# A gated mix of a spectral filter and a token MLP on one core: the row transform done first with x stationary, half the rows of the spectrum, the mirrored half made at the filter

## The chip, the cores and the metric

The kernel runs on one core of a Trainium2 chip. The metric is the time on the device in microseconds (us), the median of the runs shown. The core has five engines that each follow their own list of instructions in order and wait for one another through semaphores: TensorE (PE, with PEld for its weight loads), VectorE (DVE), ScalarE (ACT), GpSimd (POOL) and SyncE (SP, which issues all the loads and stores here).

## The reference

```python
g = sigmoid((x * gate_w).sum(-1, keepdims=True))
a = irfft2(rfft2(x) * (w_r + 1j * w_i))              # x: 1 x 2048 x 512, w: 2048 x 257
h = layernorm(x)                                     # over the 512 columns
u = gelu(einsum("bsd,sf->bdf", h, w1) + b1)          # w1: 2048 x 1792
b = (einsum("bdf,fs->bds", u, w2) + b2).transpose(0, 2, 1)
out = g * a + (1 - g) * b                            # 2048 x 512, bfloat16
```

The rows s (2048) are mixed by both parts: by the row transform of a, and by the two matrix products of b. Inputs and output are bfloat16.

## The kernel before, in words

Row s is split as 512q + 4a + r, with a on the 128 partitions, so that x is 16 tiles j = 4q + r of 128 x 512. The two products of the MLP are 14 blocks ft of 128 hidden units: `m1` (L462) sums 16 tiles of x into each block (224 matmuls of 128x512), GELU (L475, ACT) makes the block's activations `gl`, `m2` (L696) sums 14 blocks into each of the 16 output tiles (224 matmuls).

The spectral part is a chain of transforms beside this. For each tile, DVE folds x (`fold`, L361, L362), PE transposes it in 128x128 blocks (`tr`, L376), ACT copies the transposes out of PSUM (`tev`, L382), and PE transforms the columns (`f1`, L390). DVE makes the first radix-4 step over the rows (`radix4`, L413 to L429), PE makes the 128-point part (`f3`, L442 to L444), and a second radix-4 step gives the whole spectrum of 2048 x 256 in `Z`, in two halves h (even and odd columns). DVE multiplies by the complex filter (`mult`, L617 to L620). Columns 0 and 256 share a place, and POOL with three small matmuls takes them apart (`c0a`, `perm`, `c0b`, L520 to L609; 32 elements in a partition). Then the way back: radix-4, PE (`i1`, L637, L638), radix-4, and the column transform (`i3`, L665). ACT scales by the gate (L673, L675), and DVE adds to the MLP's output.

The order of all this is written out ahead of time. `Plan.order` takes each piece of work with an estimated duration, a priority and its inputs, plays it through, and the instructions are emitted in the resulting order. At run time each engine keeps that order: where a piece is late, all that stands behind it on its engine waits. In the priorities the spectral chain stands ahead of the MLP on PE, so that MLP matmuls fill the gaps. `m2` has four PSUM banks (`acc`). SP issues the loads in the plan's order, from eight that are under way at a time.

ACT loads a table of functions when it first needs one: for the copies, for Sqrt (`sq`, L346), for GELU and for Sigmoid (L491).

Of the kernel before, what the change touches and what calls it, by code (L numbers as in the profile page):

```python
# [16 lines left out]
P = 128  # L17
S = 2048
# [5 lines left out]
H = 128  # L24
# [6 lines left out]
def make_tables():  # L31

    p = np.arange(P)
    ident = np.eye(P)
    flip = np.zeros((P, P))
    flip[1:, 1:] = np.eye(P - 1)[::-1]
    e00 = np.zeros((P, P))
    e00[0, 0] = 1.0
    flip2 = np.eye(P)[::-1]
    small = bf(np.stack([flip, e00, flip2], 1))  # L40

    tf = np.zeros((P, 4, 2 * H))
    for kt in range(4):
        d = (kt % 2) * P + p[:, None]
        l = 2 * np.arange(H)[None, :] + kt // 2
        th = 2 * np.pi * ((d * l) % D) / D
        tf[:, kt, :H] = np.cos(th)
        tf[:, kt, H:] = -np.sin(th)
        if kt < 2:
            tf[:, kt, H] = np.where(d[:, 0] % 2 == 0, 1.0, -1.0)  # L50

    r4 = np.arange(4)
    ph = (4 * p[:, None, None, None] + r4[None, :, None, None]) * (r4[None, None, :, None] + 4 * p[None, None, None, :])
    th = 2 * np.pi * (ph % S) / S
    fwd = np.stack([np.cos(th), np.sin(th), -np.sin(th)], 3)
    thi = th.transpose(3, 1, 2, 0)
    inv = np.stack([-np.sin(thi), np.cos(thi), np.sin(thi)], 3)

    tg = np.zeros((P, 2, 2, 2 * H))
    sc = 2.0 / (D * S)  # L60
    for h in range(2):
        l = 2 * p[:, None] + h
        th = 2 * np.pi * ((l * np.arange(2 * H)[None, :]) % D) / D
        tg[:, h, 0] = sc * np.cos(th)
        tg[:, h, 1] = -sc * np.sin(th)
    tg[0, 0, 0] = sc / 2
    tg[0, 0, 1] = np.where(np.arange(2 * H) % 2 == 0, 1.0, -1.0) * sc / 2
    return {"ident": bf(ident), "small": small, "tf": bf(tf), "fwd": bf(fwd), "inv": bf(inv), "tg": bf(tg)}
# [123 lines left out]

@with_exitstack
def kernel(
# [25 lines left out]
    NWS = 7  # L220
    NT = 3
# [7 lines left out]
    caps = {"tp": 1, "fa": 3, "acc": 4, "xf": 2, "xT": 3, "w": NWS, "tb": NT}  # L229
# [6 lines left out]

    def load(key, shape, dt, src, nbytes, prio=0.0):
        def emit():
            t[key] = sb(shape, dt, key)
            dma(t[key][:], src)  # L240
        return add("SP", 0.2, emit, writes=[key], prio=prio, nbytes=nbytes)

    def alloc_first():
        t["x"] = sb([P, 4, 4, D], BF16, "x")
        t["h"] = sb([P, 4, 4, D], BF16, "h")
        t["xdt"] = sb([P, 4, 4, 2, 2, H], BF16, "xdt")
        t["fwd"] = sb([P, 4, 4, 3, P], BF16, "rot")
        t["Z"] = sb([P, 2, 4, 2, 4, H], BF16, "Z")
        t["gl"] = sb([P, NFT, D], BF16, "gl")
        t["pq"] = sb([P, 2048], BF16, "pq")  # L250
        t["st"] = sb([P, 2048], BF16, "st")
        t["wd"] = sb([P, 2, 2, NJ, H], BF16, "wd")
        t["wn"] = sb([P, 2, 2, NJ], BF16, "wn")
        t["wq"] = sb([P, 3, 4, 2, 2, 4], BF16, "wq")
        t["wp"] = sb([P, 2, 2, NJ], F32, "wp")
        t["wh"] = sb([P, 2, 2, NJ], F32, "wh")
        t["ghc"] = sb([P, 2, 2, NJ], F32, "ghc")
        t["u0"] = sb([P, 2, NJ], BF16, "u0")
        t["ur"] = sb([P, 2, 2, 4], BF16, "ur")
        t["us"] = sb([P, 3, 2, 4], BF16, "us")  # L260
        t["up"] = sb([P, 2, NJ], F32, "up")
        t["ct"] = sb([P, 4, 2, NJ], F32, "ct")
        t["consts"] = sb([P, 1], F32, "consts")
        for name, shape in (("stats", [P, NJ, nc.vector.BN_STATS_DIM]), ("mv", [P, NJ, nc.vector.BN_AGGR_DIM]),
                            ("rstd", [P, NJ]), ("glog", [P, NJ]), ("g", [P, NJ]), ("omg", [P, NJ]),
                            ("ombb2", [P, NJ]), ("b1f", [P, NFT]), ("b2f", [P, NJ])):
            t[name] = sb(shape, F32, name)
        V.memset(t["consts"][:], 1e-5)

    a0 = add("DVE", 0.1, alloc_first, writes=["consts"], prio=-1)  # L270


    def ld(key, dst, src, nbytes, prio):
        keys = key if isinstance(key, list) else [key]
        return add("SP", 0.2, lambda: dma(dst(), src), writes=keys, prio=prio, nbytes=nbytes, after=[a0])

    for r in range(4):
        for b in range(2 if r == 0 else 1):
            qs = slice(2 * b, 2 * b + 2) if r == 0 else slice(0, 4)
            ld([("x", r, b)] + ([("x", r, 1)] if r else []), lambda qs=qs, r=r: t["x"][:, qs, r, :], x4[:, qs, r, :],  # L280
               262144 if r == 0 else 524288, 2 * r + 0.1 * b)
# [12 lines left out]
    for r in range(4):  # L294
        for i in range(2):
            add("SP", 0.2, ld_w1(i, r), writes=[("w1", i, 4 * q + r) for q in range(4)], prio=2 * r + 0.5 + 0.1 * i,
                alloc=["w"] if r == 0 else (), nbytes=262144)
    load("ident", [P, P], BF16, tabs["ident"], 32768, prio=-1)
    load("tf", [P, 4, 2 * H], BF16, tabs["tf"], 262144, prio=0.3)
    load("small", [P, 3, P], BF16, tabs["small"], 98304, prio=14)  # L300
    for r in range(4):
        ld(("fwd", r), lambda r=r: t["fwd"][:, r, :, 0:2, :], tabs["fwd"][:, r, :, 0:2, :], 262144, 9 + r)
    load("b1b", [P, NFT], BF16, B_b1.rearrange("(t f) -> f t", f=P), 65536, prio=10.5)
    load("b2b", [P, 4, 4], BF16, B_b2.rearrange("(q a r) -> a q r", q=4, r=4), 16384, prio=10.6)
    load("gw", [P, D], BF16, gate_w[None, :].to_broadcast([P, D]), 131072, prio=13)

    def ld_wraw(comp):
        def emit():
            t["wraw", comp] = sb([P, 4, 4, 257], BF16, ("wraw", "wiaw")[comp])
            dma(t["wraw", comp][:], (A_w_r, A_w_i)[comp].rearrange("(e c k) l -> c e k l", e=4, k=4))  # L310
        return emit

    for i in range(2, NW):
        add("SP", 0.8, ld_w1(i, None), writes=[("w1", i, q) for q in range(NJ)], prio=11.5 if i == 2 else 18 + i, alloc=["w"],
            nbytes=1048576)
        if i in (3, 4):
            add("SP", 0.2, ld_wraw(i - 3), writes=[("wraw", i - 3)], prio=18.5 + i, nbytes=1056768)


    for r in range(4):  # L320
        xk = [("x", r, 0), ("x", r, 1)]
        js = [4 * q + r for q in range(4)]
        for b in range(2):
            jb = js[2 * b:2 * b + 2]

            def bn(jb=jb):
                for j in jb:
                    V.bn_stats(out=t["stats"][:, j, :], in_=t["x"][:, j // 4, j % 4, :])  # L328
                for j in jb:
                    V.bn_aggr(out=t["mv"][:, j, :], in_=t["stats"][:, j, :])  # L330
            add("DVE", 2 * (d1(512) + 0.09), bn, reads=[("x", r, b)], writes=[("mv", r, b)], prio=1.2 * r)

        def col(name, r, b):
            v = t[name][:].rearrange("p (q r) -> p q r", r=4)
            return v[:, b, r] if isinstance(b, slice) else v[:, 2 * b:2 * b + 2, r]


        for b in ((0, 1) if r == 0 else (slice(0, 4),)):
            bs = [b] if r == 0 else [0, 1]
            mvk = [("mv", r, c) for c in bs]  # L340
            rk = [("rstd", r, c) for c in bs]

            def sq(r=r, b=b):
                v = t["mv"][:].rearrange("p (q r) c -> p q r c", r=4)
                v = v[:, 2 * b:2 * b + 2, r, 1] if r == 0 else v[:, :, r, 1]
                A.activation(col("rstd", r, b), v, ActF.Sqrt, bias=t["consts"][:, 0:1], scale=1.0)  # L346
            add("ACT", 0.25, sq, reads=mvk + ["consts"], writes=rk, prio=-1)
            add("DVE", 0.12, lambda r=r, b=b: V.reciprocal(col("rstd", r, b), col("rstd", r, b)), reads=rk, writes=rk,
                prio=1.2 * r - 0.2)
        for q, j in enumerate(js):  # L350
            add("DVE", 0.32, lambda j=j: V.tensor_scalar(t["h"][:, j // 4, j % 4, :], t["x"][:, j // 4, j % 4, :], t["mv"][:, j, 0:1],
                                                         t["rstd"][:, j:j + 1], op0=Alu.subtract, op1=Alu.mult),
                reads=[("x", r, q // 2), ("rstd", r, q // 2), ("mv", r, q // 2)], writes=[("h", j)], prio=1.2 * r - 0.1)

        for b in ((0, 1) if r == 0 else (None,)):
            def fold(r=r, b=b):
                if not b:
                    t["xf", r] = t["gl"][:, 6 + 4 * (r % 2):10 + 4 * (r % 2), :].rearrange("p q (k d) -> p q k d", k=4)
# [418 lines left out]
```

## Time and profile before

| What | us |
|---|---|
| median of 3 runs (lowest, highest) | 150.26 (149.88, 150.59) |
| span of the profiled execution, first to last instruction | 148.3 |
| what lies around the span, against the median | 2.0 |
| PE, DVE, ACT, POOL busy | 132.9, 96.4, 86.9, 13.5 |
| first instruction on data (DVE, L361) | 5.06 |
| first matmul (L376), last matmul of `m1`, last matmul of `m2` | 5.55, 86.4, 144.2 |

A time of the profiled execution on its own, outside its span, is not given, so the 2.0 us around the span are the median less the span. Busy times are of one execution; a matmul's record lasts longer than the time by which it holds up the next, so the cost of a matmul is taken from the distance of starts in a run of them, not from its record.

### The profile page before, as it was taken

How to read it: one execution, taken by the hardware profiler on the slowest of the kernel's cores; microseconds unless marked ns; L12 is line 12 of the kernel's file. 1: busy time of each engine (PE TensorE's matmuls, PEld its weight loads, DVE VectorE, ACT ScalarE, POOL GpSimd, SP SyncE). 2: the span in 40 equal slices, each digit the busy share in tenths (PEclk: the TensorE clock that was granted, in tenths of full speed). 3: DMA queues.
4: the chain of work that ended last, by engine and by line, in shares of the span. 5: the costliest groups of instructions: out<-in, count | busy, mean ns of one | idle time of the engine just before them, and what ended most of it. 6: DMA issues, size and time to landing. Idle time of an engine off the chain costs nothing.

```text
span 148.3 us, 2049 instructions
## 1 busy us (share of the span) xinstructions
PE 132.9 (90%) x744; PEld 75.6 (51%) x758; DVE 96.4 (65%) x201; ACT 86.9 (59%) x165; POOL 13.5 (9%) x34
## 2 busy tenths in 40 slices
PE   0389799997996999999999999999999999999980
PEld 0155465665652444444756455676576555555530
DVE  0679989999791997694059999963988421121130
ACT  3194282797999999992831158997199111311100
POOL 0000000000063059900000000000000000000000
PEclk9999999999999999999999999999999999999998
DMA  3999969999999999454306234000003003003111
GB/s 108 271 338 319 296 92 277 291 329 324 356 298 308 399 432 400 131 214 133 150 0 201 82 92 196 0 0 0 0 12 136 0 0 141 0 0 146 70 36 38
DMA packets 26058, 24.53 MB, mean 165 GB/s; under 512 B 3392, under 2 KB 22336, under 8 KB 25920
## 3 DMA queue, kind: packets, MB, share of 16 engines
q1 hardware_dynamic: 26048, 24.40, 52.3%
q8 instruction: 6, 0.10, 0.3%
q14 instruction: 4, 0.03, 0.1%
HBM read 22.30 MB, written 2.10 MB: 164 GB/s over the span
## 4 chain that ended last, share of the span: by engine, by line
PE 68%; ACT 15%; DMA 6%; DVE 4%; POOL 2%; issue 1%; SPq 1%; ACTq 0%; POOLq 0%
PE acc L696 29%; PE acc L462 22%; ACT xT L382 5%; DMA w<-in_B_w_dram 4%; PE fa L665 4%; ACT Z L449 3%; PE fa L390 3%; PE tp L376 3%; PE fa L637 3%; PE fa L638 2%; DMA x<-in_A_x_dram 2%; ACT gl L475 2%; ACT xdt L394 2%; ACT wd L504 1%; PE fa L442 1%
## 5 line engine op out<-in xcount | busy, mean ns | idle before, releaser
L462 PE MATMUL acc<-h,w 128*128 128x512 bf16 x216 | 50.9, 383 | 0.2
L696 PE MATMUL acc<-gl,w 128*128 128x512 bf16 x218 | 49.9, 379 | 0.3
L696 PEld LDWEIGHTS <-w 128*128 128x128 bf16 x224 | 25.3, 113 | 21.0 <-DMA w<-in_B_w_dram 0.3
L462 PEld LDWEIGHTS <-w 128*128 128x128 bf16 x224 | 21.9, 99 | 23.4 <-issue 1.0
L475 ACT ACTIVATE gl<-acc,b1f 128x512 bf16<-128x512 f32 x14 | 9.7, 697 | 12.8 <-PE acc L462 12.7
L382 ACT COPY xT<-tp 128x1024 bf16<-128x1024 bf16 x8 | 8.1, 1012 | 9.8 <-PE tp L376 9.7
L376 PE MATMUL tp<-ident,gl 128*128 128x128 bf16 x64 | 5.9, 242 | 7.7 <-DVE gl L361 5.5
L725 ACT ACTIVATE tb<-acc,omg 128x512 bf16<-128x512 f32 x6 | 4.1, 687 | 14.0 <-PE acc L696 14.0
L730 DVE TENSOR_TENSOR x<-x,tb 128x512 bf16<-128x512 bf16 x6 | 2.5, 425 | 15.1 <-ACT tb L725 15.1
L413 DVE TENSOR_TENSOR pq<-xdt 128x1024 bf16<-128x1024 bf16 (+1 forms) x6 | 5.2, 860 | 10.6 <-ACT xdt L644 9.8
L390 PE MATMUL fa<-tf,xT 128*128 128x256 bf16 x64 | 10.3, 309 | 1.5 <-ACT xT L382 1.4
L449 ACT CAST Z<-fa 128x512 bf16<-128x512 f32 x16 | 8.8, 623 | 2.7 <-PE fa L444 2.7
L328 DVE BATCH_NORM_STATS2 stats<-x 128x6 f32<-128x512 bf16 x16 | 10.2, 676 | 0.0
L489 ACT ACTIVATE x<-x 128x512 bf16<-128x512 bf16 x16 | 9.9, 640 | 0.0
L376 PEld LDWEIGHTS <-gl 128*128 128x128 bf16 x64 | 4.8, 108 | 9.3 <-DVE gl L361 5.5
L707 ACT ACTIVATE x<-acc,omg 128x512 bf16<-128x512 f32 x8 | 5.5, 691 | 6.2 <-PE acc L696 6.2
L394 ACT CAST xdt<-fa 128x512 bf16<-128x512 f32 x16 | 8.8, 603 | 0.7 <-PE fa L390 0.7
L665 PE MATMUL fa<-tg,xdt 128*128 128x256 bf16 x64 | 8.8, 272 | 0.1
L390 PEld LDWEIGHTS <-xT 128*128 128x128 bf16 x64 | 6.4, 108 | 4.4 <-ACT xT L382 2.9
L644 ACT CAST xdt<-fa 128x512 bf16<-128x512 f32 x16 | 8.1, 617 | 0.0
L673 ACT ACTIVATE h<-fa,ombb,g 128x256 bf16<-128x256 f32 x16 | 7.6, 571 | 1.0 <-DVE ombb L496 1.0
L665 PEld LDWEIGHTS <-xdt 128*128 128x128 bf16 x64 | 6.3, 98 | 2.9 <-issue 0.4
(98 smaller groups left out, 170.5 us busy)
## 6 DMA issues: line engine op xcount, KB each, us to landing
w<-in_B_w_dram SPq DMA_DIRECT2D x28, 256.0 KB, 6.4
w<-in_B_w_dram SPq DMA_DIRECT2D x7, 1024.0 KB, 6.0
x<-in_A_x_dram SPq DMA_DIRECT2D x3, 512.0 KB, 6.6
rot<-dft_inv SPq DMA_DIRECT2D x1, 1536.0 KB, 12.6
out_dram<-x SPq DMA_DIRECT2D x3, 512.0 KB, 4.1
wraw<-in_A_w_r_dram SPq DMA_DIRECT2D x1, 1028.0 KB, 7.2
wiaw<-in_A_w_i_dram SPq DMA_DIRECT2D x1, 1028.0 KB, 8.4
rot<-dft_fwd SPq DMA_DIRECT2D x4, 256.0 KB, 6.1
```

Source lines behind the costliest of these rows:

```text
L328: V.bn_stats(out=t["stats"][:, j, :], in_=t["x"][:, j // 4, j % 4, :])
L376: T.transpose(tp[:, jj, k, :], t["xf", r][:, 2 * b + jj, k, :], t["ident"][:])
L382: A.copy(t["xT", i][:], t["tp", i][:])
L390: T.matmul(p1[:, k // 2], lhsT=t["xT", i][:, jj, k, :], rhs=t["tf"][:, k, :], start=(k % 2 == 0), stop=(k % 2 == 1))
L394: add("ACT", act(512), lambda q=q, r=r: A.copy(t["xdt"][:, r, q].rearrange("p c h l -> p h c l"), t["f1", q, r][:]), reads=[("f1", q, r)], ...
L449: A.copy(t["Z"][:, :, r, :, k0, :].rearrange("p h c l -> p c h l"), t["f3", k0, r][:])
L462: T.matmul(t["u", ft][:], lhsT=t["w1", ft // 2][:, j // 4, j % 4, (ft % 2) * P:(ft % 2 + 1) * P], rhs=t["h"][:, j // 4, j % 4, :], start=( ...
L475: gelus.append(add("ACT", act(512, 1), lambda ft=ft: A.activation(t["gl"][:, ft, :], t["u", ft][:], ActF.Gelu_apprx_tanh, bias=t["b1f"][:, ...
L489: A.activation(t["x"][:, q, r, :], t["x"][:, q, r, :], ActF.Copy, accum_out=t["glog"][:, 4 * q + r:4 * q + r + 1])
L644: A.copy(t["zt"][:, h, 2 * kp:2 * kp + 2, :, r, :], t["i1", h, r, kp][:])
L665: T.matmul(p3[:, jj], lhsT=t["zt"][:, h, q, comp, r, :], rhs=t["tg"][:, h, comp, :], start=(comp == 0), stop=(comp == 1))
L696: T.matmul(t["y", j][:], lhsT=t["w2", ft // 2][:, ft % 2, 512 * q + r:512 * q + 512:4], rhs=t["gl"][:, ft, :], start=(ft == 0), stop=(ft = ...
```

## The change

The spectral part is written anew; the MLP's matmuls, the tiles of x and the plan stay. In the order of the work:

- Before the data, PE multiplies zeros 13 times (`warm`), and ACT makes one Sqrt (`presq`). Most of the layernorm's scaling (`h`) goes from DVE to ACT (12 of 16 tiles).
- The rows are transformed first. DVE makes the radix-4 step over q on x itself (`q4a`, `q4b`), and PE takes x as the stationary operand against a table (`fa`), which gives the result transposed: there are no transposes by PE. Since x is real, only 1024 of the 2048 row frequencies are made, in two sets lt. Then DVE makes the radix-4 step over the columns (`d4a`, `d4b`) and over r (`radix4`), with the columns 0 and 256 taken apart by POOL (`sp0`, `sp1`), and PE makes the 128-point column part (`fb`). Sums and differences of real parts are in `B`.
- The filter is loaded in 24 pieces instead of 2; one half of it is mirrored by 16 matmuls with a flipped identity (`wf`) and copied to `W` by ACT (`wfe`). `wprep` on POOL halves one row of `W` and must be done before the first multiplication.
- DVE makes the mirrored half of the spectrum (`bfly`), multiplies both halves (`mul`, `comb`), and joins them again (`ob`).
- Row frequency 1024 lies in partition 0 of set 0 and is treated by itself: `nyq` (5 instructions) and `abf` (12 instructions) on POOL, each of up to 512 elements in one partition, and `abcopy` on DVE, which puts the result into `B`. The first inverse matmuls (`i1` of set 0) read that.
- `i1` takes the rows of `B` with step 2, `fq` on DVE joins the sets, `i3` makes both column halves of a tile, ACT scales it (512 elements), and DVE makes the sums.
- The gate uses Tanh in place of Sigmoid.

```diff
-            def tr(i=i, r=r, b=b):
-                tp = t["tp", i] = ps([P, 2, 4, P], BF16, "tp", 1)
-                for jj in range(2):
-                    for k in range(4):
-                        T.transpose(tp[:, jj, k, :], t["xf", r][:, 2 * b + jj, k, :], t["ident"][:])
...
+    def warm():
+        pw = ps([P, D], F32, "fa", 2)
+        for _ in range(NWARM):
+            T.matmul(pw[:], lhsT=t["warm"][:, 0:P], rhs=t["warm"], start=True, stop=True)
...
+            def fa(r=r, dq=dq):
...
+                T.matmul(pa[:, 0, :, 0:64], lhsT=w(0), rhs=ta[:, 0:128], start=True, stop=True)
+                T.matmul(pa[:, 0, :, 64:128], lhsT=w(1), rhs=ta[:, 128:256], start=True, stop=True)
+                T.matmul(pa[:, 1], lhsT=w(2), rhs=ta[:, 256:512], start=True, stop=False)
+                T.matmul(pa[:, 1], lhsT=w(3), rhs=ta[:, 384:640], start=False, stop=True)
...
+                def fb(lt=lt, e=e, c=c, tag=tag):
...
+                    T.matmul(pb[:, :, 0, :], lhsT=w(0), rhs=tbl(0, c), start=True, stop=True)
+                    T.matmul(pb[:, :, 2, :], lhsT=w(1), rhs=tbl(1, c), start=True, stop=True)
+                    for k in (2, 3):
+                        T.matmul(pb[:, :, 1::2, :], lhsT=w(k), rhs=tbl(k, c), start=(k == 2), stop=(k == 3))
...
+    def wprep():
+        W, pm = t["W"], t["wpm"]
+        G.tensor_scalar_mul(W[0:1, :, 0, 0, :, 0:257], W[0:1, :, 0, 0, :, 0:257], 0.5)
...
+                for i in range(2):
+                    G.tensor_mul(na[:, i], v, wn[:, i, None, 0:L].to_broadcast([1, 2, L]))
+                G.tensor_sub(nn[:, 0], na[:, 0, 1], na[:, 1, 0])
+                G.tensor_add(nn[:, 1], na[:, 1, 1], na[:, 0, 0])
+                G.tensor_mul(nn[:, :, 0], t["c0"][0:1, 0, 0, 1, :], wn[:, 0, 0:257:256])
...
+        def bfly(lt=lt):
+            b = t["B"][:, lt]
+            xs = xph(0).rearrange("p (e s l) -> p e s l", e=4, s=4)
+            V.tensor_sub(xs[:, :, 0:4:3, :], b[:, :, 0:2, :], b[:, :, 2:4, :])
+            V.tensor_add(xs[:, :, 1:3, :], b[:, :, 1::-1, :], b[:, :, 3:1:-1, :])
...
+                V.tensor_mul(o, xs, w)
+            add("DVE", tt(4096), mul, reads=["xs", ("W", comp), ("W~", comp, lt)], writes=[("pp", "st")[comp]], prio=pr)
...
+        def comb(lt=lt):
+            y, pp, qq = (v.rearrange("p (k c l) -> p k c l", k=8, c=2) for v in (xph(0), xph(1), t["st"][:]))
+            V.tensor_sub(y[:, :, 0], pp[:, :, 0], qq[:, :, 1])
+            V.tensor_add(y[:, :, 1], qq[:, :, 0], pp[:, :, 1])
...
+        def ob(lt=lt):
...
+            V.tensor_add(m[:, :, 0], y[:, :, 0], y[:, :, 1])
+            V.tensor_sub(m[:, :, 1, 0], y[:, :, 0, 1], y[:, :, 1, 1])
+            V.tensor_sub(m[:, :, 1, 1], y[:, :, 1, 0], y[:, :, 0, 0])
...
+            def abf():
...
+                G.tensor_add(nt, m[:, 0, 0], nn)
+                G.tensor_sub(nn, m[:, 0, 0], nn)
+                G.tensor_sub(d, m[:, 2, 0], m[:, 3, 0])
+                G.tensor_add(u, m[:, 2, 1], m[:, 3, 1])
+                G.tensor_add(ab[:, 0, 0], nt, m[:, 1, 0])
+                G.tensor_sub(ab[:, 2, 0], nt, m[:, 1, 0])
+                G.tensor_sub(ab[:, 1, 0], nn, m[:, 1, 1])
+                G.tensor_add(ab[:, 3, 0], nn, m[:, 1, 1])
+                G.tensor_add(ab[:, 0, 1], m[:, 2, 0], m[:, 3, 0])
+                G.tensor_sub(ab[:, 2, 1], m[:, 2, 1], m[:, 3, 1])
+                G.tensor_sub(ab[:, 1, 1], d, u)
+                G.tensor_add(ab[:, 3, 1], d, u)
...
+        if lt == 0:
+            abcopy = add("DVE", 1.15, lambda: V.tensor_copy(t["B"][0:1, 0].rearrange("p e s l -> p (e s l)"),
+                                                   t["ab"].rearrange("p r c n -> p (r c n)")),
+                reads=["ab"], writes=[("T", 0, 0), ("T", 0, 1)], prio=pr)
...
+                            T.matmul(p1[:, v], lhsT=t["B"][:, lt, r, 2 * c + v, h:L:2], rhs=tab, start=(c == 0), stop=(c == 1))
```

In the order that the plan now gives, the first `i1` matmul stands on PE behind all 224 matmuls of `m1` and 75 of `m2`; the other 149 of `m2` stand between and behind the `i1` and `i3` matmuls. On DVE, set 1 (`bfly` to `ob`) and the first step of the inverse `radix4` of set 0 stand between the `ob` of set 0 and its last steps, and `abcopy` follows these. On POOL, `abf` stands last, behind `wprep`, two `c0b` of six small instructions each, and `nyq`.

## The prediction

> **What bounds the kernel now.** I read three views in this order: the page's busy times, the page's chain that ended last, and the busy times by stage.
>
> On the page (busy us, share of the span, instructions; then the chain's shares):
>
> ```profile
> span 148.3 us, 2049 instructions
> ...
> PE 132.9 (90%) x744; PEld 75.6 (51%) x758; DVE 96.4 (65%) x201; ACT 86.9 (59%) x165; POOL 13.5 (9%) x34
> ...
> PE 68%; ACT 15%; DMA 6%; DVE 4%; POOL 2%; issue 1%; SPq 1%; ACTq 0%; POOLq 0%
> ```
>
> PE is the bound. The table by stage says where it is not (stretch, its length, busy us of each engine with instructions, clock, DMA):
>
> ```profile
> 5.50:12.50 7.00, 5.60 (x33) 3.79 (x34) 6.22 (x20) 5.23 (x8) 0.00 (x0) 1.00 1.10 324
> 12.50:48.50 36.00, 32.30 (x216) 19.37 (x219) 31.25 (x78) 26.71 (x45) 4.05 (x10) 1.00 1.06 288
> 48.50:86.40 37.90, 37.58 (x199) 19.29 (x202) 28.18 (x34) 25.09 (x56) 9.25 (x20) 1.00 0.54 207
> 86.40:112.70 26.30, 26.09 (x161) 16.87 (x163) 21.33 (x43) 21.16 (x45) 0.00 (x0) 1.00 0.17 60
> 144.20:148.30 4.10, 0.00 (x0) 0.00 (x0) 0.74 (x1) 0.00 (x0) 0.00 (x0) 0.83 0.10 34
> ```
>
> From 48.5 on PE is full: whenever the spectral chain is late, MLP matmuls stand ready. Only before 12.5 and, by 3.7 us, up to 48.5 does it wait. So a change gains by less PE work or an earlier start, and loses if PE, which keeps its written order, meets a spectral matmul whose data are late.
>
> **PE's work.** From the chain's runs of matmuls, start to start: 128 columns 0.057 us (8 transposes in 0.46), 256 columns 0.109 (8 in 0.87), 512 columns 0.216 (24 in 5.18). Before: 64 x 0.057 + 224 x 0.109 + 464 x 0.216 = 128.3. After: 64 x 0.057 (half of `fa`, `fb`) + 208 x 0.109 (the other half, 16 mirror matmuls, 64 `i1`, 64 `i3`) + 448 x 0.216 = 123.1. So 5.2 us less work, without the 13 zero matmuls ahead of the data.
>
> **The start.** The first half tile of x landed at 5.04, behind 288 KB of tables that now go; I put it at 3.6 and the second at 4.6 (they landed 1.2 apart). DVE then makes statistics (1.4), four TENSOR_TENSORs (1.8) and two small ones: first `fa` at 7.0. The Sqrt table load (1.28 on the chain at 7.77) goes from the path. The early matmuls ran at half speed (x8 in 1.89 at 10.80, later x8 in 1.04):
>
> ```profile
> 10.80 1.89 PE L390 MATMUL fa<-tf,xT 128*128 128x256 bf16 x8 [0.25 <-ACT xT L382]
> 18.75 1.04 PE L390 MATMUL fa<-tf,xT 128*128 128x256 bf16 x8
> ```
>
> With the zeros PE has been busy since about 1.1. I let it be at full speed from 7.0; if not, the first microseconds cost up to 1.1 more, hidden by a wait: the second half of the first x tiles' `h` is at the end of a DVE queue at about 12.0, where PE stands from 11.0.
>
> **The spectral chain, up to POOL.** Now each engine's list is followed with durations from rows. (1) PE from 7.0: 89 `m1` (19.2) and 16 `fa` (0.33 each, 5.3), 2.3 of waits (1.0 for `h`, 1.3 for PSUM copies behind a table load and GELUs on ACT): last `fa` copied out at 33.8. (2) DVE: `d4a`, `d4b` 1.9; four gate products 1.15 each (L484); two radix-4 steps of 4.7 (2 x 1.14 + 4 x 0.60); small ones 1.1: 50.8. (3) ACT: `fb` of set 0 waits behind a GELU, W copies and a gate (2.4), then 8 copies of 0.57: 57.8. (4) ACT: three W copies, GELU, a small copy, 2.6: 60.4; POOL's `wprep` (1028 elements in one partition) 1.2: 61.6. That product has no row; bounds are 0.8 (copies: 0.6 ns an element) and 2.3 (two inputs: 2 ns). By their sizes, 12.4 MB of loads stand in SP's queue up to the end of the 24 filter pieces, 11.2 MB up to the filter's end before; at 290 GB/s the 42.1 at which it was there becomes 46, with more issues up to 50, ahead of its use from 48 on. Behind these pieces in SP's queue are the tables of the way back and `w2`, needed from 72 on: 20 us of cover.
>
> PE is at the last mirror matmul at 58.2 and needs 64 x 0.216 + 75 x 0.216 = 30.0 to the first `i1`: **88.2**.
>
> **What POOL does to DVE.** This is where I expect the time to go. In the spectrum's filter stage the rows stand so (start, length; POOL first, then DVE):
>
> ```profile
> 57.55 0.58 POOL L555 TENSOR_TENSOR ghc<-wh 128x32 f32<-128x32 f32 x1
> 58.09 1.29 POOL L556 TENSOR_TENSOR ghc<-wh 128x32 f32<-128x32 f32 x1
> 59.47 1.22 POOL L557 TENSOR_SCALAR ghc<-ghc 128x64 f32<-128x64 f32 x1
> 60.78 0.52 POOL L601 TENSOR_TENSOR ct<-u,ghc 128x32 f32<-128x32 bf16 x1
> 62.12 0.24 POOL L604 TENSOR_TENSOR ct<-up,ghc 128x32 f32<-128x32 f32 x1
> 62.33 0.21 POOL L606 TENSOR_TENSOR ct<-ct 128x16 f32<-128x16 f32 x1
> ```
>
> ```profile
> 57.29 0.73 DVE L620 TENSOR_TENSOR Z<-st,pq 128x1024 bf16<-128x1024 bf16 x1
> 58.05 1.22 DVE L617 TENSOR_TENSOR pq<-Z,wd 128x2048 bf16<-128x2048 bf16 x1
> 59.19 1.27 DVE L618 TENSOR_TENSOR st<-Z,wd 128x2048 bf16<-128x2048 bf16 x1
> 60.50 0.69 DVE L619 TENSOR_TENSOR Z<-pq,st 128x1024 bf16<-128x1024 bf16 x1
> ```
>
> A POOL instruction of 0.24 takes 1.29 when a DVE TENSOR_TENSOR runs: L556 ends at 59.38, 0.11 after L617 at 59.27; L557 0.23 after L618. One POOL instruction gets through for each of DVE's. And DVE pays: its next instruction comes 0.04 to 0.12 late, about 2 ns for each element of POOL's 32 or 64. From 16 to 32 elements POOL's own time rises by 0.032 (2 ns an element), so one of 512 is 0.246 + 480 x 0.002 = 1.2. No row has one that long. Lower bound for what DVE loses by it: nothing (if only short ones hold it); upper: all 1.2. I take 1.0, the slope, which short ones show.
>
> The Trainium skill, SBUF — State Buffer, section "Who interferes with whom", speaks against the change: a DVE instruction with two SBUF inputs and a POOL instruction that reads SBUF share a port pair under an exclusive lock, for the whole instruction. The rows above agree for 32 to 64 elements; no row shows 512. By the rule DVE would lose all of POOL's time, and T below would be 109.
>
> The sum: (5) DVE from 61.6: product 2.3, wait for the gate 0.8, product 2.3, `comb` 2.3, first of `ob` 1.1: 70.4. The second of `ob` overwrites what `nyq` reads, and POOL has by then made 8 of its 16 instructions up to there, one for each of DVE's: 6 x 0.23 + 2 x 1.2 later it is 74.2. Two of `ob`, two half-size POOL ones, a copy: 76.8. (6) 13 DVE instructions of set 1 and the inverse step of set 0, 14.6, alternate with 12 of `abf`, 12 x 1.0: 103.4. (7) Three of 0.6 and `abcopy` (4096 elements, 1.1 from the 0.20 for 512 of L367): **T = 106.3**. PE has stood since 88.2, for 18 us; nothing covers it, since GELU and `m2` accumulators (four banks) let it no further in its order.
>
> **After T.** The order on PE leaves 35 `m2` (7.6) and 64 `i1` (7.0) to `i3`, with 1.7 of waits (the other set's radix-4, 4.7 on DVE; copies on ACT): 16.3. Then 114 `m2` (24.6), 64 `i3` (7.0) and 1.3 of waits for ACT's 0.6 a tile: 32.9. The end as before, 4.1 (last row by stage). PE wakes at half speed, as the 0.83 in that row shows 2.7 us after its last matmul: 1.2 (bounds 0, and 4 if the first 8.2 us run so, as between 5.55 and 13.8 before). Span: 106.3 + 16.3 + 32.9 + 4.1 + 1.2 = 160.8, against 148.3; with the 2.0 around the span (the median 150.26 less 148.3), **162.8**.
>
> Hidden edits: Tanh saves a table load (L491, 1.28) where ACT waits anyway; `h` on ACT (12 x 0.55) fits into ACT's gaps before 48.5 (26.7 busy of 36).
>
> **Rivals.**
> 1. *Faster: POOL and DVE do not hold each other up when POOL works in one partition.* For it: no row shows such an instruction. Against: the rows above. Then POOL does `nyq` by 69 and `abf` by 86.4, DVE reaches `abcopy`'s end at 89.7, PE waits 1.5: 89.7 + 53.3 + 2.0 = **145.0**. It decides from T under 95: 95 + 53.3 + 2.0 is 150.3.
> 2. *Same: POOL waits for DVE, but DVE loses only the 0.1 of the rows.* T = 76.8 + 14.6 + 1.2 + 2.9 = 95.5: **150.8**.
> 3. *Slower still: the filter's 24 loads land late,* since each has its own issue (0.4 to 1 us on SP): 16 after 33 would end at 50, but at 1 us each the last is at 58, and everything from (4) comes 4 later: **167**.
>
> That the change doesn't do what it says is excluded by the lists of instructions: no transposes, 16 `fa`, 16 `fb`.
>
> **How the numbers follow.** Forecast 0.67 (162.8; its own range by 0.7 to 1.2 for POOL's hold and 2 us of the start, 156 to 168), rival 1 0.15, rival 2 0.10, rival 3 0.08. The range takes in rival 2 and 3 and the forecast's bounds and leaves out most of rival 1: 147 to 169. About 0.5% is what a measurement of this kernel can tell from no change (149.88 to 150.59). Rival 2 lies near that edge and is split 0.02, 0.06, 0.02. Faster by over 0.5%: 0.17; within: 0.06; slower: 0.67 + 0.08 + 0.02 = 0.77.
>
> **What would show it.** PE idle before the first `i1` for some 18 us, ended by `abcopy`; POOL's `abf` rows ending just after DVE's rows and lasting 2 us and more; DVE's TENSOR_TENSORs between them starting 1 us late; first `fa` near 7.0 and last `fb` copy near 58. Wrong, if `abf` rows last 1.2 or less, or if DVE's rows of set 1 stand back to back beside them.

## The result and the profile after

The changed kernel takes **158.19 us** (157.39 to 159.27, 4 runs) against 150.22 us (149.88 to 150.59, 4 runs): 1.055 times as long, 95% interval 1.051 to 1.059. The profiled execution took 158.4 us, of which the span is 156.6.

The page of the kernel after (span; busy us; then PE's busy tenths and its granted clock in 40 slices; then the shares of the chain that ended last):

```profile
span 156.6 us, 2074 instructions
...
PE 132.9 (85%) x737; PEld 73.8 (47%) x737; DVE 110.9 (71%) x195; ACT 80.7 (52%) x157; POOL 57.0 (36%) x53
...
PE   6899999999999999999998000059999999999990
...
PEclk9999999999999999999999755556999999999999
...
PE 69%; DVE 22%; DMA 5%; issue 1%; ACT 1%; DVEq 0%
```

PE's busy time is that of before, but now it holds 13 zero matmuls and a stretch at half clock. The new thing is the hole: four slices of 0, with PE full before and after. On the chain DVE's share goes from 4% to 22%. PE's wait ahead of the first `i1`, and the same by stage (stretch, length, busy us of PE, PEld, DVE, ACT and POOL, clock, DMA):

```profile
PE fa L764 <- DVE B L749: 17.9, 1, 17.9
```

```profile
6.50:12.50 6.00, 5.04 (x32) 2.75 (x32) 5.48 (x20) 2.63 (x7) 0.00 (x0) 1.00 1.07 343
...
90.00:102.00 12.00, 0.00 (x0) 0.00 (x0) 12.00 (x9) 0.00 (x0) 11.01 (x7) 0.50 0.00 0
102.00:125.00 23.00, 21.41 (x136) 14.60 (x137) 13.78 (x24) 13.25 (x24) 0.00 (x0) 0.86 0.01 1
```

From 6.5 on PE works 5.0 of 6.0 us at full clock, as forecast: its four 128x512 matmuls from 9.96 on take 0.87. (The clock column alone does not show that: it reads 1.00 from 0 to 12.5 in `no_warm16` below too, where such matmuls start 0.43 apart.) From 90 to 102 only DVE and POOL work, DVE without a gap on 9 instructions, POOL on 7 up to 101.0. L749 is `abcopy`. So the balance is: work of PE 128.3 before and 123.1 after (the prediction's count); beside it 148.3 - 128.3 = 20.0 us before, and 156.6 - 123.1 = 33.5 after. Of the latter 7.0 lie ahead of the first `fa`, 17.9 are the hole, 3.6 follow the last matmul, and about 5 are half clock and small waits. Without the hole, 5.2 us of work and 4.4 us beside it were saved; the hole took these 9.6 back and 8.3 more.

### The profile page after: what moved, and what is told of

Read it like the earlier page. It is cut to its first block, busy times and chain, and to the rows that moved or that the text cites. A ratio compares the mean times of both kernels' runs of the same rounds, so it can differ in the third digit from the quotient of the medians.

```text
span 156.6 us, 2074 instructions
## 1 busy us (share of the span) xinstructions
PE 132.9 (85%) x737; PEld 73.8 (47%) x737; DVE 110.9 (71%) x195; ACT 80.7 (52%) x157; POOL 57.0 (36%) x53
## 4 chain that ended last, share of the span: by engine, by line
PE 69%; DVE 22%; DMA 5%; issue 1%; ACT 1%; DVEq 0%
PE acc L579 26%; PE acc L815 21%; PE fb L579 4%; PE fa L764 3%; DMA w<-in_B_w_dram 3%; PE fb L764 2%; PE fb L804 2%; PE fa L804 2%; DVE st L702 2%; DVE xp L702 2%; DMA x<-in_A_x_dram 2%; DVE stats L402 2%; DVE xp L708 1%; DVE xp L490 1%; DVE st L491 1%; DVE xp L707 1%
## 5 line engine op out<-in xcount | busy, mean ns | idle before, releaser
L828 ACT ACTIVATE x<-acc,ombb,omg 128x512 bf16<-128x512 f32 x14 | 10.5, 776 | 25.5 <-PE acc L815 25.5
L764 PE MATMUL fa<-rot,B 128*128 128x256 bf16 x32 | 6.0, 327 | 17.9 <-DVE B L749 17.9
L764 PEld LDWEIGHTS <-B 128*128 128x128 bf16 x64 | 6.7, 107 | 20.8 <-DVE B L749 18.4
L770 ACT CAST X<-fa 128x512 bf16<-128x512 f32 x8 | 5.1, 641 | 19.2 <-PE fa L764 19.2
L834 DVE TENSOR_TENSOR x<-x,es 128x512 bf16<-128x512 bf16 x14 | 5.6, 421 | 11.5 <-ACT x L828 11.4
L457 ACT CAST X<-fa 128x512 bf16<-128x512 f32 x16 | 8.8, 585 | 2.5 <-PE fa L454 2.3
L422 ACT ACTIVATE h<-x,nmr,rstd 128x512 bf16<-128x512 bf16 x12 | 9.0, 804 | 1.8 <-DVE nmr L417 1.8
L579 PE MATMUL fb<-h,w 128*128 128x512 bf16 x32 | 9.5, 379 | 0.0
L809 ACT ACTIVATE eo<-fa,g 128x512 bf16<-128x512 f32 x8 | 5.5, 693 | 3.4 <-PE fa L804 2.0
L804 PEld LDWEIGHTS <-xp 128*128 128x128 bf16 x64 | 6.2, 98 | 2.2 <-issue 0.5
L809 ACT ACTIVATE eo<-fb,g 128x512 bf16<-128x512 f32 x8 | 5.6, 695 | 0.9 <-DVE x L841 0.9
```

The costliest lines, as they stand in the source:

```text
L422: add("ACT", act(512, 2), lambda j=j: A.activation(t["h"][:, j // 4, j % 4, :], t["x"][:, j // 4, j % 4, :], ActF.Identity, bias=t["nmr"][ ...
L457: add("ACT", act(512), lambda r=r, dq=dq: A.copy(t["X"][:, :, r, :, dq, :], t["pa", r, dq][:]), reads=[("pa", r, dq)], writes=[("X", r, dq ...
L579: T.matmul(t["u", ft][:], lhsT=t["w1", ft // 2][:, j // 4, j % 4, (ft % 2) * P:(ft % 2 + 1) * P], rhs=t["h"][:, j // 4, j % 4, :], start=( ...
L764: T.matmul(p1[:, v], lhsT=t["B"][:, lt, r, 2 * c + v, h:L:2], rhs=tab, start=(c == 0), stop=(c == 1))
L804: T.matmul(p3[:, h], lhsT=z[:, q, v, r, :], rhs=t["tg"][:, h, v, :], start=(v == 0), stop=(v == 1))
L809: A.activation(t["eo", j][:], t["i3", j][:], ActF.Copy, scale=t["g"][:, j:j + 1])
```

## The experiments

Theory: `nyq` and `abf`, 512 elements in one partition on POOL, and DVE's two-input operations hold each other up; so DVE brings T (the end of `abcopy`) late, and PE, whose written order was made with shorter times, stands. Rivals: DVE's own work in this order sets T; the loss goes by the number of POOL's instructions; the work behind T is not bound by PE, so that filling the hole buys nothing. Each kernel was timed in 4 runs beside the kernel before; the ratios are to that. T and PE's stand are from the profile; the table gives T as the start of the first `i1`, some 0.05 after `abcopy` ends.

| Kernel | T | PE stands | us | ratio (95%) |
|---|---|---|---|---|
| after | 103.5 | 17.9 | 158.19 | 1.055 (1.051 to 1.059) |
| `row_short` | 90.0 | 4.5 | 144.65 | 0.959 (0.951 to 0.967) |
| `plan_known` | 103.6 | 3.9 | 143.97 | 0.958 (0.950 to 0.965) |
| `row_dve16` | 92.2 | 1.2 | 138.92 | 0.925 (0.920 to 0.930) |
| `idle_mm` | 103.4 | 7.6 | 157.63 | 1.050 (1.043 to 1.058) |
| `after_chain` | 103.6 | 18.1 | 157.36 | 1.052 (1.047 to 1.056) |
| `wprep_dve` | 100.9 | 15.7 | 156.46 | 1.044 (1.039 to 1.050) |
| `idle_mm84` | 103.8 | 0 | 156.51 | 1.045 (1.041 to 1.049) |
| `both_dve16` | 91.8 | 1.9 | 139.70 | 0.933 (0.928 to 0.938) |
| `row_dve16b` | 92.4 | 1.2 | 139.03 | 0.925 (0.920 to 0.930) |
| `no_warm16` | 94.0 | 1.2 | 140.45 | 0.934 (0.928 to 0.939) |
| `no_presq16` | 92.1 | 1.2 | 139.04 | 0.925 (0.921 to 0.930) |
| `row_dve` | 95.9 | 1.3 | 140.21 | 0.933 (0.929 to 0.938) |

**`row_short`: POOL's operations made short.**

```diff
-                G.tensor_sub(d, m[:, 2, 0], m[:, 3, 0])
+                G.tensor_sub(d[:, 0:8], m[:, 2, 0, 0:8], m[:, 3, 0, 0:8])
```

(so for all of `abf` and `nyq` but the last, which has 2 elements already; `abcopy` becomes two copies.)

> Of the row of frequency 1024 only 8 of 512 elements are computed (its five products and sums in nyq and its twelve in abf stay 17 GpSimd instructions, each on 8 elements), and the final copy of that row reads another tile, so this row of the result is left out; every instruction's place in the written order is that of the kernel after. Theory (VectorE's two-input operations and the 512-element GpSimd operations hold each other up for the length of the operation): VectorE's filter operations fall back to 2.3, 1.22 and 0.68 us, T (end of the row's copy, 103.5 in the kernel after) comes 12.6 us of lengthened operations and about 3 us of waiting for GpSimd earlier, at 88 to 89, TensorE (at work until 85.3) stands 2 to 5 us and not 18.3, and the time is 141 to 145 us. Rival one (a fixed loss per GpSimd instruction, whatever its length): the lengthening stays at about 0.85 to 1 us per VectorE operation, T at 98 or later, time 153 or more. Rival two (VectorE's own work in this order is the limit, GpSimd only runs beside it): T and time within 1 us of the kernel after, 157 to 159.

144.65 us, T 13.5 us earlier: as the theory has it, and the first two rivals fall. T itself comes at 90.0, a us later than I had put it. The rows show how the hold works. In the kernel after, POOL's and then DVE's instructions of one stretch (start, length):

```profile
84.01 2.12 POOL L731 TENSOR_TENSOR X<-B 1x512 f32<-1x512 bf16 x1
86.10 2.12 POOL L732 TENSOR_TENSOR X<-X,B 1x512 bf16<-1x512 f32 x1
```

```profile
83.06 2.06 DVE L707 TENSOR_TENSOR xp<-xp,st 128x2048 bf16<-128x2048 bf16 x1
85.05 2.17 DVE L708 TENSOR_TENSOR xp<-st,xp 128x2048 bf16<-128x2048 bf16 x1
```

The same in `row_short`, with 8 elements:

```profile
78.79 1.17 POOL L732 TENSOR_TENSOR X<-X,B 1x8 bf16<-1x8 f32 x1
79.93 1.17 POOL L733 TENSOR_TENSOR X<-X,B 1x8 bf16<-1x8 f32 x1
81.07 0.19 POOL L734 TENSOR_TENSOR X<-X,B 1x8 bf16<-1x8 f32 x1
```

```profile
78.65 1.26 DVE L707 TENSOR_TENSOR xp<-xp,st 128x2048 bf16<-128x2048 bf16 x1
79.83 1.21 DVE L708 TENSOR_TENSOR xp<-st,xp 128x2048 bf16<-128x2048 bf16 x1
```

A POOL instruction of 8 elements, 0.19 when it gets through at once, still takes 1.17: it waits out one of DVE's. But DVE's take 1.21 to 1.26, hardly more than the 1.21 that L490 needs at 89.88, where POOL has nothing to do. With 512 elements both take over 2: each waits out the other's turn. The ends of DVE's stretch, in the kernel after and then in `row_short`:

```profile
74.34 1.21 DVE L694 TENSOR_TENSOR xp<-B 128x2048 bf16<-128x2048 bf16 x1
...
101.49 0.68 DVE L506 TENSOR_TENSOR B<-st 128x1024 bf16<-128x1024 bf16 x1
102.27 1.22 DVE L749 COPY B<-X 1x4096 bf16<-1x4096 bf16 x1
```

```profile
71.73 1.22 DVE L694 TENSOR_TENSOR xp<-B 128x2048 bf16<-128x2048 bf16 x1
...
87.75 0.69 DVE L506 TENSOR_TENSOR B<-st 128x1024 bf16<-128x1024 bf16 x1
```

From the start of set 1's `bfly` (L694) to the end of the last radix-4 step (L506) DVE needs 27.8 us (74.34 to 102.17) in the kernel after and 16.7 (71.73 to 88.44) here: 11.1 for 12 `abf` operations, **0.93 each**. So the loss goes by the length of POOL's operation, not by the count. In `row_dve16` below, with no `abf` on POOL, the same stretch takes 20.6, of which DVE's own 12 `abf` operations are 4.15: 16.4 are left, so a POOL operation of 8 elements, 0.19 long, costs DVE only some 0.03.

**`plan_known`: the planner told the true length of `abf`.** Here and in `row_dve16` the `i1` groups are also chained in their order (the edit of `after_chain`).

```diff
-            add("POOL", pool_(512, 12), abf, reads=bk + ["nn"], writes=["ab"], prio=0)
+            add("POOL", 25.3, abf, reads=bk + ["nn"], writes=["ab"], prio=0)
```

> The computation is the kernel after's; only the planner is told 25.3 us in place of 9.2 for the twelve abf operations (what they took on the chip), and the i1 groups are chained in their order. It then writes 140 in place of 75 of the 14x16 output matmuls (L815) ahead of the first i1 matmul. Theory (TensorE stands 18 us because its written order is fixed with too short an abf): T stays at 102 to 105, 65 matmuls of 0.215 us = 14 us move into the gap, TensorE stands 3 to 6 us, the time falls by 10 to 14 us to 144 to 148. Rival (the work after T is bound by ScalarE's copies and VectorE's sums and not by TensorE, so that matmuls moved ahead buy little): gap filled, but the stretch from T to the end shrinks by less than 5 us, time 153 to 158.

T stays at 103.6, PE arrives 14 us later and stands 3.9: 143.97 us, just below what was expected. The rival falls: the work behind T was bound by PE. So the late T cost so much only because the order was written for an earlier one. PE around T in `plan_known`:

```profile
103.58 1.03 PE L764 MATMUL fa<-rot,B 128*128 128x256 bf16 x4 [3.92 <-DVE B L749]
104.41 5.77 PE L815 MATMUL acc<-gl,w 128*128 128x512 bf16 x14
```

14 matmuls of 512 columns in 5.77 are 0.41 each, not 0.216: after 3.9 us without work PE is at half clock (0.50 in the clock column from 102.8 to 109.6).

**`row_dve16`: the row on DVE, in bf16.**

```diff
-                G.tensor_add(nt, m[:, 0, 0], nn)
+                V.tensor_add(nt, m[:, 0, 0], nn)
...
-            add("POOL", pool_(512, 12), abf, reads=bk + ["nn"], writes=["ab"], prio=0)
+            add("DVE", 12 * tt(512), abf, reads=bk + ["nn"], writes=["ab"], prio=0)
```

> The row of frequency 1024 (nyq and abf) is computed on VectorE in bf16 instead of GpSimd in f32; the i1 groups are chained in their order, and the planner, with these costs, puts 100 output matmuls ahead of the first i1. Theory (mutual hold): VectorE takes on 17 operations of 1x512, each 0.34 to 0.68 us from the 128x1024 rows (6 to 12 us), and loses 12.6 us of hold and 3 us of waiting: T at 93 to 98, TensorE arrives at 85.3 + 25 x 0.215 = 90.7 and stands 2 to 8 us, time 145 to 151. Rival (VectorE's own work in this order is the limit): the 17 operations come on top, T at 109 to 115, time 160 or more.

138.92 us, below the range expected, and **0.925 (0.920 to 0.930) of the kernel before**. DVE's rows of `abf` and PE's wait ahead of `i1`:

```profile
73.70 0.41 DVE L732 TENSOR_TENSOR X<-B 1x512 bf16<-1x512 bf16 x1
74.04 0.41 DVE L733 TENSOR_TENSOR X<-X,B 1x512 bf16<-1x512 bf16 x1
```

```profile
PE fa L765 <- DVE B L750: 1.2, 1, 1.2
```

They start 0.34 apart: the 12 cost DVE 4.1 us, where on POOL they took 25.3 and cost DVE 11.1; and the 5 of `nyq` lie where DVE waited for `wprep`. Of the 19.5 us of span won over the kernel after, 11.4 are T and 8.1 what follows it: 25 matmuls more ahead of `i1` (25 x 0.216 = 5.4), no half clock (about 2.0, below), and 0.7 that I did not trace.

**`idle_mm` and `idle_mm84`: the hole filled with matmuls,** 48 and 84 of them, ahead of the first `i1`.

```diff
+                    if (h, r, lt) == (0, 0, 0):
+                        for _ in range(48):
+                            T.matmul(p1[:].rearrange("p a b c -> p (a b c)"), lhsT=t["flip"][:], rhs=t["h"][:, 0, 0, :], start=True, stop=True)
```

> The kernel after with 48 more 128x512 matmuls (results overwritten) written ahead of the first i1 matmul, 48 x 0.377 = 18.1 us, about what TensorE stands. Theory (after the 18 us without work the granted clock is 0.5 until about 110 and this costs 1 to 3 us): clock about 1.0 from 103 on, first i1 where it was or up to 0.5 later, the stretch from T to the end 1 to 3 us shorter, time 155 to 157.5. Rival (i1 is bound by ScalarE's copies, the clock costs nothing): stretch unchanged, time 158 to 159.

It did not test what it was to test: I had taken the length of a matmul's record (0.377) for its step (0.216), so PE still stood 7.6 us and woke at half clock, and 157.63 is just above the range.

> As idle_mm with 84 in place of 48 filling matmuls: each took 0.22 us there, not 0.377, so that they ended 7.7 us ahead of T; 84 x 0.216 = 18.1 us now covers the whole gap. Theory (the stand of TensorE costs more than its own length, because the first 5 us or so after it run at half clock): no matmul at 0.427 us after T, the stretch from T to the end 1.5 to 2.5 us shorter than in the kernel after, time 155.5 to 157. Rival (ScalarE's copies bind the i1 stage, the clock costs nothing): stretch unchanged, 158 to 159.

Now the clock holds. PE of the kernel after, then of `idle_mm84`:

```profile
106.51 3.35 PE L815 MATMUL acc<-gl,w 128*128 128x512 bf16 x10
```

```profile
105.50 2.32 PE L818 MATMUL acc<-gl,w 128*128 128x512 bf16 x9
```

From the first `i1` to the end it is 154.9 - 103.8 = 51.1 us in place of 53.1. The clock costs 2.0 us of the span (1.7 between the medians), as expected. `idle_mm` lies between: by the clock column its half clock lasts 3.2 us from the first `i1` on, in the kernel after 5.1, and the same stretch takes 52.1. So the 2.0 holds for the profiled execution; what a stand costs varies with how long the half clock happens to last.

**`after_chain`: the control.**

```diff
-                add("PE", mm(*[256] * 4), i1, reads=[("T", lt, r % 2), "ti"], writes=[("i1", h, r, lt)], prio=3, alloc=[tag])
+                add("PE", mm(*[256] * 4), i1, reads=[("T", lt, r % 2), "ti"], writes=[("i1", h, r, lt), "i1s"], prio=3, alloc=[tag])
```

> The kernel after with its i1 groups chained in their order, and nothing else: VectorE, ScalarE, GpSimd and the loads keep their written order, and 75 output matmuls still stand ahead of the first i1. It is the control for the two runs in which the chain was needed. Theory: the chain is worth nothing by itself, T at 103 to 104, TensorE stands 18 us, time within 1 us of 158.2. Rival (the order of the i1 groups after T is what gained in those runs): 3 us or more faster, 155 or less.

157.36, within 1 us of the kernel after, and the intervals overlap: the chain did not make the gains of 14 and 19 us.

**`wprep_dve` and `both_dve16`: the halving of one row of W on DVE.**

```diff
-        G.tensor_scalar_mul(W[0:1, :, 0, 0, :, 0:257], W[0:1, :, 0, 0, :, 0:257], 0.5)
+        V.tensor_scalar_mul(W[0:1, :, 0, 0, :, 0:257], W[0:1, :, 0, 0, :, 0:257], 0.5)
```

(and the two sums of `wprep` behind it.)

> The kernel after with the three operations of wprep on VectorE in place of GpSimd, each at its old place in the written order. Theory (the 1x1028 scaling on GpSimd, 2.82 us, is on the way to T in full): VectorE needs 0.3 to 0.5 us for it (from 1.22 us for its 1x4096 copy) and about 0.2 for each of the two 128x16 operations, its first filter product starts at about 58.3 and not 60.3, and GpSimd reaches the c0 products 3 to 5 us earlier, so that VectorE's wait of 3.0 us for them shrinks as well: T 2 to 5 us earlier, time 153 to 156.2. Rival (GpSimd's part after it, which is held up by VectorE, sets T): T unchanged, 157.5 to 158.5.

POOL's row in the kernel after, and DVE's group in `wprep_dve` (count; busy us, mean ns):

```profile
57.46 2.82 POOL L649 TENSOR_SCALAR W<-W 1x1028 bf16<-1x1028 bf16 x1 [0.95 <-ACT W L642]
```

```profile
L649 DVE TENSOR_SCALAR W<-W 1x1028 bf16<-1x1028 bf16 x1 | 0.4, 414 | 0.0
```

T comes 2.6 us earlier and the span is 2.0 shorter: `wprep` was on the path, but of DVE's 3.0 us of waiting for POOL at L715 only 2.1 go, so the time, 156.46, lies just outside what was expected (156.2).

> row_dve16 with wprep on VectorE too; the planner, with these costs, puts 94 output matmuls ahead of the first i1. Theory: the first filter product starts 2 us earlier, T at 89.5 to 91 in place of 92, TensorE arrives at 89.5 and stands 0 to 1.5 us; from there TensorE's own work is the limit, so that at most the 1.4 us it stood in row_dve16 is gained: 137 to 138.7 us against 138.9. Rival (VectorE still ends late, each operation on it moves T by its length): 139 or more.

No gain on top of `row_dve16` (139.70, 0.933 with its interval from 0.928, against 0.930 at most): with `nyq` on DVE its wait for `wprep` was 0.4 us, T moves by 0.4 only, and the planner puts 94 instead of 100 matmuls ahead of `i1`, so that PE stands 1.9. I had called at most 1.4 us a gain; the rival's time comes nearer, though T did not move later as it says.

**The start: `row_dve16b`, `no_warm16`, `no_presq16`.** In `row_dve16` PE works without a hole, so that a loss at the start reaches the end.

```diff
-    add("PE", 0.42 * NWARM, warm, reads=["warm", "xs"], writes=["warmed"], prio=-5, alloc=["fa"], free=["fa"])
```

```diff
-    add("ACT", 1.5, presq, reads=["eps"], writes=["omg"], prio=-5)
```

> The kernel of row_dve16 once more, as the base of the three others of this call: 138.5 to 139.5 us; T at 92, TensorE stands 1.4 us ahead of i1.

> row_dve16 without the 13 zero matmuls at the start; every other instruction keeps its place. There TensorE is at work 95% of the span, so that a loss at the start reaches the end. Theory (as predicted: they put the clock at full speed ahead of the first fa at 7.0; without them up to 1.1 us is lost at half clock, 0.5 to 0.9 of it in the wait for h that follows): first fa stays at 6.9 to 7.1, it and its neighbours take about 0.43 per 512 columns for the next microseconds, time 0 to 0.6 us above row_dve16. Rival (the clock needs longer from work with gaps than from a run of matmuls): half clock to beyond 14, time 2 us or more above.

> row_dve16 without the early square root that loads ScalarE's table before the data is there; every other instruction keeps its place. Theory: the load of 1.28 us then stands ahead of the first rstd, VectorE waits that much longer for it, h and (where the sums of x stand behind it on VectorE) the first fa come up to 1.3 us later, time 0.6 to 1.3 us above row_dve16. Rival (the load fits ahead of the data or is hidden by TensorE's work on fa): within 0.4 us.

Without the zeros the time is 1.4 us more (140.45 against 139.03, timed together): more than I expected, less than the rival's 2. The first `fa` stays at 6.9; two early matmuls of 512 columns without and with the zeros:

```profile
8.36 1.06 PE L577 MATMUL acc<-h,w 128*128 128x512 bf16 x2
```

```profile
7.69 0.59 PE L579 MATMUL acc<-h,w 128*128 128x512 bf16 x2
```

Without the zeros PE is at half clock until 12.5. Its last matmul ahead of `i1` starts 1.6 later (92.4 against 90.8), and the wait for `h`, 0.8 with the zeros, is gone: that hides a third of the loss. T is 1.6 later too: PE's mirror matmuls, ACT's copies and `wprep` behind them all move (`wprep` starts at 59.22 in place of 57.58). Without the early Sqrt nothing changes (139.04), and the theory falls: the table load stands at 0.72 all the same, since Sqrt is then ACT's first function of all.

```profile
0.72 1.28 ACT L411 ACT_TABLE_LOAD   x1 [0.72 <-PEq L872]
```

In the kernel before, ACT's first function was another and the load of Sqrt's table came at 7.77; so I read it that the change removed this load by taking the copies of transposes away, not by `presq`; no kernel here has the copies and `presq`.

**`row_dve`: the row on DVE in f32.** The edit is that of `row_dve16` without bf16 and without the chain; the planner is given 0.60 us for each operation.

> nyq and abf on VectorE as in row_dve16, but in f32 as GpSimd had them; without the chain, and with the longer durations the planner is given it puts 117 output matmuls ahead of the first i1. Theory (the gain is from the hold that goes, not from bf16): the 1x512 operations take 0.41 to 0.85 us with f32 operands, T at 92 to 97, TensorE arrives at 94.3 and stands 0 to 3 us, time 139 to 142. Rival (bf16 made the gain): operations of 1.1 us as on GpSimd, T at 100 or later, time 146 or more.

140.21 us: operations of 0.67 (bf16 0.41), T at 95.9, 117 matmuls ahead of `i1`. Most of the gain is that of the hold; bf16 adds little (1.2 us between the two kernels, which differ also in the chain and the plan).

## Why the prediction was right, and where its sizes were off

- **The mechanism and the place hold.** PE stands 17.9 us (18 forecast) ahead of the first `i1`, ended by `abcopy`; `abf` rows last 1.6 to 3.2; DVE's operations between them are 0.85 to 1.06 longer; the first `fa` is at 6.99 (7.0). `row_short` takes the hold away and the slowdown is gone.
- **Steps (1) and (2)** are met: last `fa` copied out 33.75 (33.8), radix-4 done at 50.4 (50.8).
- **Step (3) was too late:** `fb`'s last copy at 55.2, not 57.8. I gave ACT's copies 0.57 each; their records last 0.6 to 0.7, but they start 0.48 apart.
- **Step (4), `wprep`, was mis-sized:** 1.2 (bounds 0.8 and 2.3), measured 2.82, outside the bounds. The two errors partly cancel: DVE goes on at 60.3 (61.6).
- **Steps (5) to (7):** 69.0, 72.0, 74.3 (70.4, 74.2, 76.8): 1.4, 2.2 and 2.5 too late, 1.3 of it from (4) and the rest mostly from the wait for `nyq`, 3.0 and not 3.8. From there to T 29.2 us (29.5). The 1.0 for each `abf` operation was 0.93. In DVE's wait for `nyq` POOL's two operations of 512 took 2.15, so one alone is about 1.08 (1.2 by the slope). The Trainium skill, SBUF — State Buffer, section "Who interferes with whom", calls the lock on the shared port pair exclusive, and says of DVE's two-port modes that it is held for the whole instruction: DVE's loss of 0.93 out of 1.08 agrees in kind, the 0.03 out of 0.19 of `row_short` does not, and I was wrong to say that the rows before agree (0.04 to 0.12 lost to instructions of 0.24 and more). By these numbers some 0.15 us of POOL's operation costs DVE nothing. That the hold is one of ports no run here shows. The 109 that I worked out by the rule for T was 5.5 too late: 2.5 through the terms ahead of it, some 3 through the price of an operation (1.2 for 0.93).
- **PE's arrival** was 85.6, not 88.2: the waits up to `fb` were shorter than allowed (last mirror matmul at 55.5, not 58.2). So T 2.8 earlier and PE 2.6 earlier leave the hole nearly as forecast: that it was right to 0.1 us is the luck of two errors of a size.
- **After T:** 53.1, where 16.3 + 32.9 + 4.1 + 1.2 = 54.5 were forecast. The clock took 2.0 (1.2, bounds 0 and 4), the end 3.6 (4.1), the rest 47.5 (49.2). Around the span 1.6, not 2.0, counted in the same way. Together: 158.2, not 162.8.
- **"Nothing covers the hole"** failed. I wrote that GELU and the four accumulator banks let PE go no further in its order. The order does stop it there, but not the banks: `plan_known` puts 65 more matmuls ahead of `i1` and wins 14 us.
- **The zeros** were put at up to 1.1 us, hidden by the wait for `h`: they are worth 1.4 us beyond what that wait hides, measured in `row_dve16`; in the kernel after itself I did not take them out. Rivals 1 and 2 fall by the rows of DVE; of rival 3, the last filter load was issued by 49.97, and no engine waited for one. Of the hidden edits none was taken out by itself; ACT now loads two tables in place of four, and PE works 37.49 of the 37.5 us from 12.5 to 50, so that `h` on ACT holds nothing up there.

## What to carry to other kernels

Work that looks free because it is small and on an idle engine must be asked what it shares: 12 operations in one partition on POOL cost DVE 0.93 us each and PE most of an 18 us stand; on DVE itself they cost 0.34 each. When an order is written by a planner, a wrong duration costs time on other engines, which are ordered around it: `abf` was given as 9.2 us and took 25.3, and the right number alone was worth 14 us. Give the planner the duration measured next to the neighbours, not alone. And read a loss of a change apart from its idea: with the row on DVE the same change makes the kernel 7.5% faster than before.

## What was not expected of the hardware

- A short one-input operation of DVE is held up too: the cast of 128x16 (L720) takes 1.15 beside `abf` and 0.20 in `row_short`.
- POOL's scaling of 1028 bf16 elements in one partition takes 2.82 us, DVE's 0.41.
- PE's clock: stands of 1.2 and 1.9 us (`both_dve16`) leave it at full speed, stands of 3.9, 4.5, 7.6 and 18 us do not; by the clock column it fell 2.5 us after the last matmul in the kernel after and 4.4 us after it in `after_chain`. Afterwards 512 columns take 0.427 us instead of 0.216, for 3.2 us (`idle_mm`), 3.3 (`after_chain`), 5.0 (`row_short`), 5.1 (after), 5.7 (`wprep_dve`) or 6.0 (`plan_known`), and for 5.6 at the start without zeros. The Trainium skill, TensorE: Matmul & The Clock Gate, section "What's actually happening", puts the idle window at about 3.4 us: the 2.5 and 4.4 lie on both sides of it, so as a fixed limit it does not hold here.
